# Talking-heads attention with a squared-ReLU FFN: GpSimd queue in written order, weights in eight spread loads, longer score bursts, column-tiled work bundled

## The chip, the cores and the metric

The kernel runs on one core of one Trainium2 chip. The metric is the device time of one execution in microseconds, the median of several runs. All times "us from the start" are from a profiled run's first instruction. With one core there is no second die to compare; a run is called slow when it is more than 1.5% above the fastest run of the same kernel. PE is TensorE, DVE VectorE, ACT ScalarE, POOL GpSimd, and SP the engine whose queue issues the gathers and stores. A name such as h_ps stands for the matmuls that write this PSUM tile.

## The reference

```python
scores = scale * np.matmul(q, k.transpose(0, 1, 3, 2))     # 8 batches, 12 heads, 448 x 64
scores = np.einsum('bhij,hg->bgij', scores, w_pre)         # mixes the heads
scores = scores - np.max(scores, axis=-1, keepdims=True)
attn = np.exp(scores)
attn = attn / (np.sum(attn, axis=-1, keepdims=True) + 1e-09)
attn = np.einsum('bhij,hg->bgij', attn, w_post)            # mixes them again
x = np.matmul(attn, v)                                     # -> (3584, 768)
h = np.maximum(x @ w_in, 0.0)                              # w_in 768 x 2048
out = h * h @ w_out                                        # w_out 2048 x 768
```

## The kernel before

A batch is cut into 45 steps of ten query rows. A step mixes the heads (`mix`: one matmul on a gathered tile G, an exp on ScalarE, a reciprocal on DVE, a normalising operation d on GpSimd) and, three steps later, mixes them back (`unmix`: four matmuls, a copy `at` on DVE). G is gathered by a DMA from the scores S, in written order six steps ahead; it has eight buffers (`AHEAD + 2`). The FFN of a batch is cut into units that serve as filler between the steps of the next batch. "share" spreads what is left of them over the rest of the batch, and single units (transposes, attention-value) are booked as debt in `owed`.

```python
LAG = 3; AHEAD = 6
...
def fill(ns):
    owed[0] += ns
    while filler and owed[0] > 0:
        w, f = filler.pop(0)
        f()
        owed[0] -= w
    if not filler:
        owed[0] = min(owed[0], 0.0)
...
with tc.manual_schedule(engines={PE}):            # the other queues are ordered by the framework
    ...                                           # transposes and scores of the first block
    for x in range(AHEAD):
        gather(steps[x])
    nc.gpsimd.dma_start(out=wpost_bf[:, :], in_=w_post[0:H, 0:H])
    vs[0] = load(v, 0, "v", 2)
    for c2 in range(NPAIR):                       # six loads of w1
        nc.gpsimd.dma_start(out=w1[c2][:, :], in_=moe_w_in[c2 * 128:(c2 + 1) * 128, 0:DFF])
    kk = load(k, 1, "kst", 1)
    staged[1] = (load(q, 1, "qst", 1), kk)
    for ft in range(FT):                          # sixteen loads of w2
        nc.gpsimd.dma_start(out=w2[ft][:, :], in_=moe_w_out[ft * 128:(ft + 1) * 128, 0:DMODEL])
    for i in range(len(steps) + LAG):
        ...
        rest = NT - (s0[1] if s0 else 0)
        share = sum(w for w, _ in filler) / max(rest - 1, 1) / 2 if s0 else 1e9
        now = timed.pop(i, [])
        if s0: mix(s0)
        for w, f in now:
            f()
            owed[0] -= w
        fill(share)
        if s1: unmix(s1)                          # queues attention-value units for i+1, i+2
        if i + AHEAD < len(steps): gather(steps[i + AHEAD])
        ...                                       # score bursts of two pairs at tiles 0, 2, 4
        fill(share)
```

The softmax here doesn't subtract the row's maximum and nothing guards it: scores larger than these inputs give would overflow.

Of the kernel before, what the change touches and what calls it, by code (L numbers as in the profile page):

```python
# [8 lines left out]
BF16 = mybir.dt.bfloat16  # L9
# [3 lines left out]
PE = mybir.EngineType.PE  # L13
# [17 lines left out]
LAG = 3  # L31
# [6 lines left out]
def kernel(  # L38
# [27 lines left out]
    def load(src, b, name, bufs, parts=1):  # L66
        t = stage.tile([P, H, R, D], BF16, name=name, tag=name, bufs=bufs)
        n = H // parts
        for x in range(parts):
            hs = slice(n * x, n * x + n)  # L70
            nc.gpsimd.dma_start(out=t[0:PR, hs, :, :].rearrange("p h r d -> p h (r d)"),
                                in_=src[b, hs, :, :].rearrange("h (p r) d -> p h (r d)", r=R))
        return t

    staged, vs = {}, {}
    kk = load(k, 0, "kst", 1, parts=3)
    staged[0] = (load(q, 0, "qst", 1, parts=3), kk)

    ident = consts.tile([P, P], BF16, name="ident")
    masks.make_identity(nc, ident[:, :])  # L80

# [35 lines left out]
    w1 = [wts.tile([P, DFF], BF16, name=f"w1_{c2}") for c2 in range(NPAIR)]  # L117
    w2 = [wts.tile([P, DMODEL], BF16, name=f"w2_{ft}") for ft in range(FT)]
# [64 lines left out]

    def ffn1_unit(b, ft):
        ps = bank("h_ps")
        for c2 in range(NPAIR):
            nc.tensor.matmul(ps[:, 0:S], lhsT=w1[c2][:, ft * 128:(ft + 1) * 128], rhs=xts[b][:, c2, :],  # L187
                             start=(c2 == 0), stop=(c2 == NPAIR - 1))
# [18 lines left out]
    def ffn2_unit(b, mt, nt, part):  # L207
# [3 lines left out]
        for ft in range(8 * part, 8 * part + 8):  # L211
            for n2 in ((nt,) if mt < 3 else (0, 1)):
                dst = ps[:, 0:384] if mt < 3 else ps[64 * n2:64 * n2 + 64, 0:384]
                nc.tensor.matmul(dst, lhsT=h2ts[(b, ft)][:, mt * 128:mt * 128 + ROWS[mt]],  # L214
                                 rhs=w2[ft][:, n2 * 384:(n2 + 1) * 384], start=(ft == 0), stop=(ft == FT - 1))
# [25 lines left out]
    def score_burst(b, blk, pairs):  # L241
# [12 lines left out]
        for h, ps in got:  # L254
            if h % 2 == 0:
# [64 lines left out]
    with tc.manual_schedule(engines={PE}):  # L320
        for _, f in turn_units(0):
            f()
        for x in range(3):
            score_burst(0, 0, [2 * x, 2 * x + 1])
        for x in range(AHEAD):
            gather(steps[x])
        nc.gpsimd.dma_start(out=wpost_bf[:, :], in_=w_post[0:H, 0:H])
        vs[0] = load(v, 0, "v", 2)
        for c2 in range(NPAIR):
            nc.gpsimd.dma_start(out=w1[c2][:, :], in_=moe_w_in[c2 * 128:(c2 + 1) * 128, 0:DFF])  # L330
        kk = load(k, 1, "kst", 1)
        staged[1] = (load(q, 1, "qst", 1), kk)
        for ft in range(FT):
            nc.gpsimd.dma_start(out=w2[ft][:, :], in_=moe_w_out[ft * 128:(ft + 1) * 128, 0:DMODEL])
        for i in range(len(steps) + LAG):
            s0 = steps[i] if i < len(steps) else None
            s1 = steps[i - LAG] if i >= LAG else None
            if s0:
                b, t = s0
                blk, tl = divmod(t, TPB)  # L340
                if t == 0:
                    if b == 0:
                        at_step(i + 12, (100, cg_unit))
                    at_step(i + 13, (900, lambda b=b: bias_unit(b)))
                    if b + 1 < B:
                        for x, u in enumerate(turn_units(b + 1)):
                            at_step(i + 15 + 3 * x, u)
                if t == 36 and b + 2 < B:
                    kk = load(k, b + 2, "kst", 1)
                    staged[b + 2] = (load(q, b + 2, "qst", 1), kk)  # L350
                if t == 10 and b + 1 < B:
                    vs[b + 1] = load(v, b + 1, "v", 2)
# [9 lines left out]
            if s1:  # L362
                unmix(s1)
                b1, t1 = s1
                if t1 % TT == TT - 1:
                    for x, u in enumerate(av_units(b1, t1 // TT)):
                        at_step(i + 1 + x, u)
                if t1 == NT - 1:
                    filler.extend(ffn_units(b1))
            if i + AHEAD < len(steps):  # L370
                gather(steps[i + AHEAD])
            if s0:
                nxt = blocks.index((b, blk)) + 1
                first = [0, 2, 4] if blk < 3 else [0, 1, 2]
                if nxt < len(blocks) and tl in first:
                    x = first.index(tl)
                    score_burst(*blocks[nxt], [2 * x, 2 * x + 1])
# [36 lines left out]
```

## Time and profile before

| what | before |
|---|---|
| median of the first three runs | 685.85 us (685.82 to 686.61) |
| busy share of PE, DVE, ScalarE, GpSimd | 89, 62, 59, 56% |
| first mix (m_ps) | 27.1 us |
| first FFN matmul (h_ps) | 120.3 us |
| seven batch periods, first h_ps of batch 0 to that of batch 7 | 523.0 us |
| from there to the end | 41.5 us |

The last three rows add to the span. They are a start that ends with the first FFN matmul, seven periods in which attention of one batch and FFN of the previous one run together, and the last FFN alone. The boundaries are the starts of the first h_ps of each batch in the PE timeline.

### The profile page before, as it was taken

The page shows a single profiled execution, that of the slowest core. Times are in us where ns is not written, and L with a number is a line of the kernel's source. Part 1 is how long each engine was busy: PE and PEld are TensorE (multiplying, and loading weights), DVE is VectorE, ACT ScalarE, POOL GpSimd, SP SyncE. Part 2 cuts the span into 40 slices and gives each one's busy share as a digit, 9 for nine tenths or more (in the row PEclk, how much of TensorE's full clock was granted, in tenths as well). Part 3 has the DMA queues.
Part 4 walks back from the last instruction along what each step waited for, and adds up shares of the span by engine and source line. Part 5 has one row for each costly group of instructions (what it writes and reads, how often), then busy time and mean ns, then how long its engine had stood idle before and what let it go on. Part 6 is the DMA issues. An engine that isn't in the chain of part 4 may idle for free.

```text
span 684.8 us, 16963 instructions
## 1 busy us (share of the span) xinstructions
PE 609.3 (89%) x6282; PEld 367.6 (54%) x6282; DVE 426.0 (62%) x1036; ACT 404.5 (59%) x1185; POOL 382.5 (56%) x545
## 2 busy tenths in 40 slices
PE   4207977899999999999999999999999999999897
PEld 3004544466556555566656565566556565556554
DVE  4105887566677767766767767666767667675201
ACT  2205777575477656775577657775577557764330
POOL 6226455576377734874376725873387436764360
PEclk9555898999999999999999999999999999999999
DMA  9999495548474665649474766549474345434102
GB/s 149 219 201 180 75 153 96 100 65 132 110 135 79 91 139 113 116 70 154 107 132 71 95 137 119 101 76 158 110 127 72 71 87 109 72 58 96 36 0 82
DMA packets 87959, 73.47 MB, mean 107 GB/s; under 512 B 5700, under 2 KB 84036, under 8 KB 87876
## 3 DMA queue, kind: packets, MB, share of 16 engines
q1 hardware_dynamic: 51842, 49.57, 34.4%
q0 software_dynamic: 35904, 22.81, 24.4%
q8 instruction: 49, 0.80, 0.5%
q14 instruction: 34, 0.28, 0.1%
q10 hardware_dynamic: 130, 0.01, 0.0%
HBM read 45.63 MB, written 11.01 MB: 83 GB/s over the span
## 4 chain that ended last, share of the span: by engine, by line
PE 71%; DMA 17%; DVE 6%; ACT 3%; issue 1%; POOL 1%; SPq 0%; DVEq 0%; ACTq 0%; POOLq 0%
PE o_ps L214 20%; PE h_ps L187 18%; DMA G<-S 10%; PE at_ps L296 9%; PE m_ps L276 8%; PE ot_ps L170 6%; PE s_ps L251 5%; DMA qst<-in_q_dram 5%; PE tr_ps L144 3%; DVE at L298 3%; DVE S L258 2%; DMA out_dram<-osb 2%; ACT xt L178 1%; PE vs_ps L157 1%; DMA w<-in_moe_w_out_dram 1%
## 5 line engine op out<-in xcount | busy, mean ns | idle before, releaser
L283 POOL TENSOR_SCALAR d<-e_sb,rc 120x448 bf16<-120x448 f32 x360 | 228.5, 638 | 202.7 <-DVE rc L281 200.6
L298 DVE CAST at<-at_ps 112x480 bf16<-112x480 f32 x360 | 231.4, 651 | 86.5 <-PE at_ps L296 83.3
L279 ACT ACTIVATE e_sb<-m_ps 120x448 f32<-120x448 f32 x360 | 195.9, 547 | 146.3 <-PE m_ps L276 98.0
L187 PE MATMUL h_ps<-xt,w 128*128 128x448 bf16 x768 | 164.9, 354 | 0.0
L214 PE MATMUL o_ps<-w,h 128*128 128x384 bf16 (+1 forms) x1024 | 162.6, 327 | 0.0
L296 PE MATMUL at_ps<-post,d 120*128 120x120 bf16 (+1 forms) x1440 | 138.6, 220 | 22.6 <-POOL d L283 22.2
L276 PE MATMUL m_ps<-G,pre 120*120 120x448 bf16 x360 | 135.8, 377 | 25.4 <-DMA G<-S 25.0
L296 PEld LDWEIGHTS <-d 120*128 120x128 bf16 (+1 forms) x1440 | 104.5, 101 | 69.2 <-POOL d L283 26.7
L192 POOL TENSOR_TENSOR h<-hr 128x448 bf16<-128x448 f32 x128 | 119.2, 931 | 34.9 <-ACT hr L191 34.3
L214 PEld LDWEIGHTS <-h 128*128 128x128 bf16 (+1 forms) x1024 | 85.0, 101 | 54.9 <-issue 7.4
L258 DVE CAST S<-s_ps 128x448 bf16<-128x448 f32 x192 | 109.8, 614 | 3.3 <-DMA G<-S 1.6
L191 ACT ACTIVATE hr<-h_ps 128x448 f32<-128x448 f32 x128 | 69.6, 544 | 65.2 <-PE h_ps L187 60.9
L281 DVE RECIPROCAL rc<-sm 120x1 f32<-120x1 f32 x360 | 57.1, 159 | 81.6 <-ACT e_sb L279 78.3
L256 ACT CAST S<-s_ps 128x448 bf16<-128x448 f32 x192 | 92.5, 540 | 21.7 <-PE s_ps L251 21.7
L187 PEld LDWEIGHTS <-w 128*128 128x128 bf16 x768 | 70.6, 98 | 62.3 <-issue 8.8
L276 PEld LDWEIGHTS <-pre 120*120 120x120 bf16 x360 | 48.8, 136 | 67.7 <-DMA G<-S 37.1
L279 ACT ACTIVATION_READ_ACCUMULATOR e_sb<-m_ps 120x1 f32 x360 | 73.9, 205 | 0.0
L251 PE MATMUL s_ps<-kT,qT 64*128 64x448 bf16 x384 | 60.5, 375 | 1.3 <-ACT e_sb L279 0.4
L170 PE MATMUL ot_ps<-at,v 112*64 112x150 bf16 x1152 | 48.7, 236 | 12.3 <-DVE at L298 12.2
L178 ACT ACTIVATE xt<-ot_ps,bvec 128x150 bf16<-128x150 f32 (+1 forms) x144 | 44.9, 383 | 22.5 <-PE ot_ps L170 22.5
L221 DVE COPY osb<-o_ps 128x384 f32<-128x384 f32 x48 | 26.7, 556 | 49.6 <-PE o_ps L214 48.8
L170 PEld LDWEIGHTS <-v 112*64 112x64 bf16 x1152 | 41.2, 113 | 21.9 <-issue 13.4
(33 smaller groups left out, 159.6 us busy)
## 6 DMA issues: line engine op xcount, KB each, us to landing
G<-S SPq DMA_DIRECT2D x352, 105.0 KB
v<-in_v_dram POOLq DMA_DIRECT2D x8, 672.0 KB, 10.1
kst<-in_k_dram POOLq DMA_DIRECT2D x7, 672.0 KB, 8.2
qst<-in_q_dram POOLq DMA_DIRECT2D x7, 672.0 KB, 13.2
w<-in_moe_w_in_dram POOLq DMA_DIRECT2D x6, 512.0 KB, 15.9
w<-in_moe_w_out_dram POOLq DMA_DIRECT2D x16, 192.0 KB, 7.4
out_dram<-osb SPq DMA_DIRECT2D x8, 336.0 KB
out_dram<-osb SPq DMA_DIRECT2D x8, 288.0 KB
```

The source lines that it names most:

```text
L170: nc.tensor.matmul(ps[64 * hh:64 * hh + 64, TQ * y:TQ * y + TQ], lhsT=vs[b][0:PR, g, r, :], rhs=at[0:PR, r, g, :], start=(y == 0 and r == ...
L187: nc.tensor.matmul(ps[:, 0:S], lhsT=w1[c2][:, ft * 128:(ft + 1) * 128], rhs=xts[b][:, c2, :], start=(c2 == 0), stop=(c2 == NPAIR - 1))
L192: nc.gpsimd.tensor_tensor(out=h2[:, :], in0=hr[:, :], in1=hr[:, :], op=ALU.mult)
L214: nc.tensor.matmul(dst, lhsT=h2ts[(b, ft)][:, mt * 128:mt * 128 + ROWS[mt]], rhs=w2[ft][:, n2 * 384:(n2 + 1) * 384], start=(ft == 0), stop ...
L251: nc.tensor.matmul(ps[:, 0:S], lhsT=qTs[b][rs, p, BLK_START[blk]:BLK_START[blk] + P], rhs=kTs[b][rs, p, :], start=True, stop=True)
L256: nc.scalar.copy(out=sb[:, h, :], in_=ps[:, 0:S])
L258: nc.vector.tensor_copy(out=sb[:, h, :], in_=ps[:, 0:S])
L276: nc.tensor.matmul(ps[0:n, 0:S], lhsT=pre[0:n, 0:n], rhs=Gs.pop(s)[0:n, :], start=True, stop=True)
L279: nc.scalar.activation(out=e[0:n, :], in_=ps[0:n, 0:S], func=ACT.Exp, scale=SCALE, accum_out=sm[0:n, 0:1])
L283: nc.gpsimd.tensor_scalar(out=d[0:n, 0:S], in0=e[0:n, :], scalar1=rc[0:n, 0:1], scalar2=-1.0 / S, op0=ALU.mult, op1=ALU.add)
L296: nc.tensor.matmul(ps[:, RG * r:RG * r + RG], lhsT=d[0:n, PR * r:PR * r + P], rhs=post[0:n, :], start=True, stop=True)
L298: nc.vector.tensor_copy(out=ats[(b, third)][0:PR, :, :, IQ * tl:IQ * tl + IQ], in_=ps[0:PR, 0:R * RG].rearrange("p (r g i) -> p r g i", r= ...
```

## The change

Its intent is to free the GpSimd queue of weight loads that stand before compute work, to spread these loads over two batches, and to switch PE less often between full, row-tiled and column-tiled matmuls. Cut to its core:

```diff
-LAG = 3
+LAG = 4
...
+    load(staged[0][0], q, 0, 0, 4)               # k and q parts alternate
+    for x in (4, 8):
+        load(staged[0][1], k, 0, x, x + 4)
+        load(staged[0][0], q, 0, x, x + 4)
...
-    w1 = [wts.tile([P, DFF], BF16, name=f"w1_{c2}") for c2 in range(NPAIR)]
-    w2 = [wts.tile([P, DMODEL], BF16, name=f"w2_{ft}") for ft in range(FT)]
+    w1 = [wts.tile([P, NPAIR, DFF // 4], BF16, name=f"w1_{x}") for x in range(4)]
+    w2 = [wts.tile([P, FT // 4, DMODEL], BF16, name=f"w2_{x}") for x in range(4)]
...
-            if h % 2 == 0:
+            if h % 2 == 0 or (b == 0 and h in (3, 9)):
                 nc.scalar.copy(out=sb[:, h, :], in_=ps[:, 0:S])
...
-    with tc.manual_schedule(engines={PE}):
+    with tc.manual_schedule(engines={PE, POOL}):
...
+        for x in range(2):                       # block 1 is scored before the steps
+            score_burst(0, 1, [3 * x, 3 * x + 1, 3 * x + 2])
...
+        at_load(0, load_v, 0)
+        at_load(2, load_k, 1)
+        at_load(5, load_q, 1)
+        for x in range(4):
+            at_load(10 + 5 * x, load_w1, x)
+            at_load(44 + 4 * x, load_w2, x)
+        for b in range(B):
+            if b + 1 < B:
+                at_load(NT * b + 32, load_v, b + 1)
+            if b + 2 < B:
+                at_load(NT * b + 36, load_k, b + 2)
+                at_load(NT * b + 40, load_q, b + 2)
...
-                    at_step(i + 13, (900, lambda b=b: bias_unit(b)))
+                    at_step(i + 16 + LAG, (900, lambda b=b: bias_unit(b)))
-                            at_step(i + 15 + 3 * x, u)
+                            at_step(i + 16 + LAG if x < 3 else i + 31 + LAG, u)
...
-                    for x, u in enumerate(av_units(b1, t1 // TT)):
-                        at_step(i + 1 + x, u)
+                    for u in av_units(b1, t1 // TT):
+                        at_step(i + 2, u)
                 if t1 == NT - 1:
-                    filler.extend(ffn_units(b1))
+                    at_step(i + 2, (0, lambda b1=b1: filler.extend(ffn_units(b1))))
...
-                first = [0, 2, 4] if blk < 3 else [0, 1, 2]
+                first = [0, 4] if blk < 3 else [0, 2]
-                    score_burst(*blocks[nxt], [2 * x, 2 * x + 1])
+                    score_burst(*blocks[nxt], [3 * x, 3 * x + 1, 3 * x + 2])
```

More of the change, by code (lines that the diff above doesn't have):

```diff
@@ L12 @@
 ALU = mybir.AluOpType
-PE = mybir.EngineType.PE
+PE, POOL = mybir.EngineType.PE, mybir.EngineType.Pool
 B, H, S, D = 8, 12, 448, 64
@@ L62, in bank, with stage_tile, load @@
         return psp.tile([P, 512 if dtype == F32 else 1024], dtype, name=name, tag="ps")
-    def load(src, b, name, bufs, parts=1):
-        t = stage.tile([P, H, R, D], BF16, name=name, tag=name, bufs=bufs)
-        n = H // parts
-        for x in range(parts):
-            hs = slice(n * x, n * x + n)
-            nc.gpsimd.dma_start(out=t[0:PR, hs, :, :].rearrange("p h r d -> p h (r d)"),
-                                in_=src[b, hs, :, :].rearrange("h (p r) d -> p h (r d)", r=R))
-        return t
+    def stage_tile(name, bufs):
+        return stage.tile([P, H, R, D], BF16, name=name, tag=name, bufs=bufs)
+    def load(t, src, b, h0=0, h1=H):
+        nc.gpsimd.dma_start(out=t[0:PR, h0:h1, :, :].rearrange("p h r d -> p h (r d)"),
+                            in_=src[b, h0:h1, :, :].rearrange("h (p r) d -> p h (r d)", r=R))
     staged, vs = {}, {}
-    kk = load(k, 0, "kst", 1, parts=3)
-    staged[0] = (load(q, 0, "qst", 1, parts=3), kk)
+    staged[0] = (stage_tile("qst", 1), stage_tile("kst", 1))
+    load(staged[0][1], k, 0, 0, 4)
     ident = consts.tile([P, P], BF16, name="ident")
     masks.make_identity(nc, ident[:, :])
+    load(staged[0][0], q, 0, 0, 4)
+    for x in (4, 8):
+        load(staged[0][1], k, 0, x, x + 4)
+        load(staged[0][0], q, 0, x, x + 4)
     def wcol(w, name, eng):
@@ L182, in av_units, with load_v, load_k, load_q @@
         return [(800, lambda cp=cp: av_unit(b, third, cp)) for cp in range(2)]
+    def load_v(b):
+        vs[b] = stage_tile("v", 2)
+        load(vs[b], v, b)
+    def load_k(b):
+        kst = stage_tile("kst", 1)
+        load(kst, k, b)
+        staged[b] = (stage_tile("qst", 1), kst)
+    def load_q(b):
+        load(staged[b][0], q, b)
+    def load_w1(x):
+        n = DFF // 4
+        nc.gpsimd.dma_start(out=w1[x][:, :, :],
+                            in_=moe_w_in[:, n * x:n * x + n].rearrange("(c p) f -> p c f", p=P))
+    def load_w2(x):
+        n = DFF // 4
+        nc.gpsimd.dma_start(out=w2[x][:, :, :],
+                            in_=moe_w_out[n * x:n * x + n, :].rearrange("(c p) m -> p c m", p=P))
     def ffn1_unit(b, ft):
@@ L186, in ffn1_unit @@
         for c2 in range(NPAIR):
-            nc.tensor.matmul(ps[:, 0:S], lhsT=w1[c2][:, ft * 128:(ft + 1) * 128], rhs=xts[b][:, c2, :],
+            nc.tensor.matmul(ps[:, 0:S], lhsT=w1[ft // 4][:, c2, ft % 4 * 128:ft % 4 * 128 + 128], rhs=xts[b][:, c2, :],
                              start=(c2 == 0), stop=(c2 == NPAIR - 1))
@@ L214, in ffn2_unit @@
                 nc.tensor.matmul(dst, lhsT=h2ts[(b, ft)][:, mt * 128:mt * 128 + ROWS[mt]],
-                                 rhs=w2[ft][:, n2 * 384:(n2 + 1) * 384], start=(ft == 0), stop=(ft == FT - 1))
+                                 rhs=w2[ft // 4][:, ft % 4, n2 * 384:(n2 + 1) * 384], start=(ft == 0), stop=(ft == FT - 1))
         if part == 0:
@@ L319 @@
     steps = [(b, t) for b in range(B) for t in range(NT)]
-    with tc.manual_schedule(engines={PE}):
-        for _, f in turn_units(0):
-            f()
+    with tc.manual_schedule(engines={PE, POOL}):
+        first = turn_units(0)
         for x in range(3):
+            first[2 * x][1]()
+            first[2 * x + 1][1]()
             score_burst(0, 0, [2 * x, 2 * x + 1])
+        for x in range(2):
+            score_burst(0, 1, [3 * x, 3 * x + 1, 3 * x + 2])
         for x in range(AHEAD):
@@ L327, with at_load @@
         nc.gpsimd.dma_start(out=wpost_bf[:, :], in_=w_post[0:H, 0:H])
-        vs[0] = load(v, 0, "v", 2)
-        for c2 in range(NPAIR):
-            nc.gpsimd.dma_start(out=w1[c2][:, :], in_=moe_w_in[c2 * 128:(c2 + 1) * 128, 0:DFF])
-        kk = load(k, 1, "kst", 1)
-        staged[1] = (load(q, 1, "qst", 1), kk)
-        for ft in range(FT):
-            nc.gpsimd.dma_start(out=w2[ft][:, :], in_=moe_w_out[ft * 128:(ft + 1) * 128, 0:DMODEL])
+        loads = {}
+        def at_load(i, f, *args):
+            loads.setdefault(i, []).append(lambda: f(*args))
+        at_load(0, load_v, 0)
[10 more added lines that the diff above has]
+                at_load(NT * b + 40, load_q, b + 2)
         for i in range(len(steps) + LAG):
+            for f in loads.get(i, []):
+                f()
             s0 = steps[i] if i < len(steps) else None
@@ L343 @@
                         at_step(i + 12, (100, cg_unit))
-                    at_step(i + 13, (900, lambda b=b: bias_unit(b)))
+                    at_step(i + 16 + LAG, (900, lambda b=b: bias_unit(b)))
                     if b + 1 < B:
                         for x, u in enumerate(turn_units(b + 1)):
-                            at_step(i + 15 + 3 * x, u)
-                if t == 36 and b + 2 < B:
-                    kk = load(k, b + 2, "kst", 1)
-                    staged[b + 2] = (load(q, b + 2, "qst", 1), kk)
-                if t == 10 and b + 1 < B:
-                    vs[b + 1] = load(v, b + 1, "v", 2)
+                            at_step(i + 16 + LAG if x < 3 else i + 31 + LAG, u)
             rest = NT - (s0[1] if s0 else 0)
@@ L373 @@
                 nxt = blocks.index((b, blk)) + 1
-                first = [0, 2, 4] if blk < 3 else [0, 1, 2]
-                if nxt < len(blocks) and tl in first:
+                first = [0, 4] if blk < 3 else [0, 2]
+                if 1 < nxt < len(blocks) and tl in first:
                     x = first.index(tl)
-                    score_burst(*blocks[nxt], [2 * x, 2 * x + 1])
+                    score_burst(*blocks[nxt], [3 * x, 3 * x + 1, 3 * x + 2])
             if i + 1 < len(steps) + LAG:
```

## The prediction

> **What bounds the kernel now.** I read the stretch table first (busy time of each engine in windows), with the cuts set where the first FFN matmul of each batch stands in the PE timeline: 120.3, 197.0, 272.4, 347.5, 423.5, 499.3, 574.5 and 643.3 us. The columns are stretch, length, busy us of PE, PEld, DVE, ACT, POOL, granted clock, DMA share, GB/s.
>
> ```profile
> 17.00:53.00 36.00, 4.17 (x12) 0.96 (x12) 3.64 (x9) 4.03 (x11) 9.13 (x18) 0.52 1.14 208
> 53.00:120.00 67.00, 54.54 (x604) 32.55 (x605) 52.40 (x138) 48.13 (x149) 37.36 (x58) 0.82 0.71 124
> ...
> 423.50:499.30 75.80, 73.64 (x789) 44.73 (x787) 53.17 (x129) 50.07 (x149) 45.92 (x65) 1.00 0.62 110
> ...
> 643.30:685.00 41.70, 36.83 (x226) 20.42 (x224) 3.90 (x7) 9.62 (x19) 14.92 (x16) 0.99 0.12 34
> ```
>
> So there are four regimes, not one bound. From 17 to 53 us every compute engine is nearly idle and only the DMA engines are full. From 53 to 120 us no engine is full; VectorE (DVE) is the busiest, 52.4 of 67 us. From 120 to 643 us, seven batch periods, PE is 97% busy and is the bound. The last 41.7 us are the last batch's FFN alone. The page's 89% for PE averages over these.
>
> Second view, the waits between 14 and 60 us, and the POOL timeline there:
>
> ```profile
> PE at_ps L296 <- POOL d L283: 19.0, 1, 19.0
> ACT e_sb L279 <- POOL d L283: 18.9, 1, 18.9
> PEld L276 <- DMA G<-S: 16.4, 4, 11.1
> ```
>
> ```profile
> 32.35 0.53 POOL L334 DMA_DIRECT2D w<-in_moe_w_out_dram x1 [2.15 <-DMA w<-in_moe_w_in_dram]
> 39.47 0.53 POOL L334 DMA_DIRECT2D w<-in_moe_w_out_dram x1 [6.59 <-DMA kst<-in_k_dram]
> 44.75 0.53 POOL L334 DMA_DIRECT2D w<-in_moe_w_out_dram x1 [4.76 <-DMA qst<-in_q_dram]
> ...
> 52.35 0.53 POOL L334 DMA_DIRECT2D w<-in_moe_w_out_dram x1 [0.41 <-DMA w<-in_moe_w_out_dram]
> 52.91 1.86 POOL L283 TENSOR_SCALAR d<-e_sb,rc 120x448 bf16<-120x448 f32 x3
> ```
>
> The reader should see a queue blocked at its head: four exps are done by 34.4 us, but the d operation that normalises them stands in the GpSimd queue behind sixteen w2 issues, each of which waits for an earlier load to land. With three e_sb buffers, ScalarE stops too, and PE after it. Before that, the first gather (issued at 18.14 us) lands only at 27.1 us, since the loads have filled the DMA engines.
>
> Third view, the PE timeline in the PE-bound regime (start us, duration, instructions):
>
> ```profile
> 437.02 0.35 PE L276 MATMUL m_ps<-G,pre 120*120 120x448 bf16 x1
> 437.21 0.37 PE L296 MATMUL at_ps<-post,d 120*128 120x120 bf16 x4
> 437.52 0.55 PE L251 MATMUL s_ps<-kT,qT 64*128 64x448 bf16 x4
> 438.00 0.40 PE L276 MATMUL m_ps<-G,pre 120*120 120x448 bf16 x1
> 438.33 0.58 PE L144 MATMUL tr_ps<-ident,kst 112*64 112x112 bf16 x16
> 438.85 0.38 PE L296 MATMUL at_ps<-post,d 120*128 120x120 bf16 x4
> ```
>
> ```profile
> 394.04 0.97 PE L170 MATMUL ot_ps<-at,v 112*64 112x150 bf16 x24 [0.81 <-DVE at L298]
> ```
>
> Read start to start, since busy times overlap. An m_ps takes 0.19 us before a full-array matmul but 0.33 (typically 0.28) before a column-tiled one; sixteen transposes take 0.52 us before a full-array matmul, but 0.42 where another column-tiled group follows. Hence a column-tiled group standing alone costs about 0.09 us in and 0.10 out, 0.19 in all. A score burst (64 rows) shows the same: at_ps to s_ps is 0.31 against 0.21, and four score matmuls take 0.48 where two pitches of 448 columns (0.19 each, as six h_ps take 1.14) would be 0.38; 0.10 on each side, 0.20 per burst. Last, an attention-value group waits up to 0.8 us for the at copy of the step just before it.
>
> **What the Trainium skill says.** "TensorEngine Tiling (Array Packing)", Key Properties: "Mode switching requires drain". The trace agrees, with the 0.09 to 0.10 us above at each side. "PSUM — Partial Sum Buffer", Engine vs sequencer instructions: the GpSimd queue is a strict FIFO; that is the 19.0 us wait. "DMA: Bandwidth & Descriptors", Queues, rings and completion order: each DMA engine goes round between the queues it has work for, a packet at a time. The trace agrees only in part: gathers do get through while loads run, but in 17 to 53 us at a DMA share of 1.14 the first took 9 us, against 2.9 us for the one at 79.45 us in the chain of waits.
>
> **The change, part by part.**
> (1) Start. k and q parts now alternate, and the two first score blocks are computed before the steps. From 1.3 us the first k part landed at 5.4, and four parts had by 10.24, so 1.6 us a part; the sixth lands near 13.4. Its transposes and copies (0.75 + 0.62), then four score matmuls and their copies (about 1.3) put the first block's S at 16.3 us, against 18.0 now. Fewer loads compete, so a gather of about 3 us gives the first mix at 19 us rather than 27.1.
> (2) The GpSimd queue in written order. Eight weight loads of 768 KB stand between steps, so no d waits for weights. This deletes the 34.4 to 52.9 stall, about 18.5 us, and the 12 us of slow first gathers around it.
> (3) Batch 0's own pace. From mix 10 at 59.7 us to mix 50 at 115.9 the kernel takes 1.40 us a step. DVE's 52.4 us of those 67 lose the copies of block 1 (now before the steps) and two copies per block (h 3 and 9, to ScalarE): fourteen at 0.53 us (six took 3.27 us) are 7, though four more steps come into the stretch, at 0.8 each. So DVE needs some 48 us for 50 steps, 0.97 a step. The DMA engines must bring 45 gathers of 105 KB (4.7 MB), five loads of v, k and q for batches 1 and 2 (3.4 MB) and w1 (3.1 MB): 11.2 MB, at 208 GB/s (the full stretch above) 54 us. With two bundles, each some 4 us of PE work in which ScalarE and DVE run short, I take 1.22 us a step, 61 us for 50 steps. First FFN matmul at 19 + 61 = 80 us instead of 120.3: 40 us gained.
> (4) Steady batches. Column-tiled groups go from 13 a batch (bias 1, transposes 6, attention-value 6; one adjacent already) to 3 bundles: 9 x 0.19 = 1.7 us. Score bursts go from 12 to 8: 4 x 0.20 = 0.8. The attention-value wait, 12.2 us in 16 waits over eight batches, is 1.5 a batch; with two steps between I count 1.2 as gone. Sum 3.7 a batch; all of it is on PE, which sets the end here. Six periods give 22, the last one (fewer groups) 2: 24 us of 523.
> (5) Given back. Bursts of six of the eight PSUM banks and bundles that open six must wait for copies (three at about 0.44 on ScalarE, three at 0.53 on DVE, beside the exps and at copies), and w2's 3.1 MB arrive in batch 1. I put 5 us for the seven periods. LAG 4 lengthens nothing but the drain of one step.
> (6) The end: 96 and 128 matmuls alone, 41.5 us, unchanged.
> Sum: 80 + (523 - 24 + 5) + 41.5 = 625.5; the reference time is 1 us above the profiled span, but (1) and (3) lean slightly careful, so I say 624.
>
> **The rivals.**
> A: batch 0 becomes DMA-bound. The loads merely move from one clump to a belt along the whole batch, gathers land late (6 to 9 us against six steps of lookahead, that is 7 us), and the pace stays at 1.4 to 1.5 us. For it: the share of 1.14 under loads, and the 7.7 us gather at 95.6 us while v, k and q arrive. Against: w1 isn't needed before step 50 and can lag. The first FFN matmul would be at 90 to 95, the total 636 to 641.
> B: PSUM stalls eat the steady gain. Six banks at once leave two; if each of 64 bursts costs PE 0.4 us, that is 26 us, and the total is 645. For it: PE already waits at bursts now (0.16 to 0.28 us where two bursts follow closely in batch 0). Against: ScalarE and DVE are at 66 and 70% in the steady stretch, and at the PE-bound pace of 1.68 us a step three extra copies drain within two steps.
> C: batch 0 runs at the pace of DVE alone and nothing is given back: first FFN matmul at 70, periods 3.8 shorter: 70 + 499 + 41 = 610.
> D: nothing moves, since the 18.5 us stall only shifts a DMA bound: the weights still have to land before w1 is used. It would give 660 to 685. Against: all weights landed by 60 us, w1 is used at 120, so there's room.
>
> **Range and chances.** The start stall is sure to go, and even A with B keeps 25 us. Between C with some luck (606) and A with half of B (648) should lie 8 of 10. Faster by over 2% means under 672; only D threatens it: 0.96 faster, 0.03 same, 0.01 slower.
>
> **What would show each step.** (1) and (2): first m_ps near 19 us; no d waiting over 3 us for a load; PE's stretch from 20 to 60 us over 50% busy. (3): first h_ps at 74 to 92 us; if later, look at waits on G (A) or at DVE's share. (4): periods near 72 us, tr_ps, vs_ps and ot_ps contiguous in the PE timeline, "PE ot_ps <- DVE at" below 3 us. (5): waits of s_ps, m_ps or tr_ps for DVE or ScalarE copies of 5 us in all, not 26. (6): the last 128 + 96 matmuls as now. I would be wrong if periods stay at 75 us, or if the first FFN matmul comes after 100.

## The result

The changed kernel takes 660.73 us (median of four runs: 660.58, 670.95, 660.88, 657.29; the second is a slow run, at a granted clock of 0.934 against 0.956 to 0.971). The kernel before took 685.84 us in the same rounds. The ratio of the fast runs is 0.9627, 95% interval 0.9572 to 0.9683: faster by 3.7%. A ratio here is the mean time of one kernel's fast runs over that of the other's in the same rounds, so it isn't quite the ratio of the medians quoted. The direction was right, but 660.7 lies outside the range of 606 to 648; 61.8 us of gain were forecast and 25.1 came.

| part of the span | before | predicted | after |
|---|---|---|---|
| first m_ps | 27.1 | 19 | 21.5 |
| first h_ps | 120.3 | 80 | 109.2 |
| seven periods | 523.0 | 504 | 508.2 |
| the rest | 41.5 | 41.5 | 41.4 |

So most of the miss, 27 of 37 us, is in one place, between the first mix and the first FFN matmul (61 us forecast, 87.7 measured). The stretch table of the changed kernel (columns as in the prediction) shows it:

```profile
21.50:45.00 23.50, 15.64 (x79) 7.98 (x80) 9.61 (x28) 11.25 (x36) 10.82 (x16) 1.00 0.92 157
45.00:65.00 20.00, 16.36 (x237) 10.95 (x234) 14.86 (x42) 14.55 (x47) 12.38 (x19) 0.91 1.03 195
65.00:85.00 20.00, 14.86 (x176) 10.15 (x173) 14.84 (x39) 12.82 (x43) 11.11 (x18) 0.83 0.94 154
85.00:109.20 24.20, 16.42 (x137) 9.83 (x138) 13.09 (x37) 13.54 (x43) 11.07 (x18) 0.65 0.97 180
...
405.10:479.10 74.00, 71.78 (x789) 44.90 (x787) 53.40 (x129) 49.74 (x150) 45.57 (x64) 1.00 0.62 114
```

No compute engine is full from 21.5 to 109.2 us: DVE, the limit that the prediction named, is busy for 13 of 24 us at 85 to 109, and PE for at most 16.4 of 20. What stands near its limit is the DMA share, the last number but one, 0.92 to 1.03 throughout. In the kernel before it was 1.14 from 17 to 53 us and 0.71 on average from there to 120. The clock falls to 0.65 in the last stretch. The Trainium skill, "TensorE: Matmul & The Clock Gate", Part 1, states that the array goes to half clock after an idle window of about 3.4 us. This trace agrees only in part: the clock was at half from 84.9 to 102.0 us, but in the 3.4 us before that PE was busy for 1.54 us and had no gap over 1.01.

The waits of the changed kernel in its first 130 us (waiter, releaser, us in total, times, longest) show what took the place of the weights:

```profile
PEld L299 <- DMA G<-S: 30.6, 25, 6.0
PE m_ps L299 <- DMA G<-S: 22.2, 16, 5.8
...
PEld L319 <- POOL d L306: 3.1, 3, 1.3
```

The wait of PE's weight loads for d, in the kernel before 24.2 us with 19.5 in the one stall, is 3.1. The wait of PE for gathers is 22; in the kernel before it was 7 from 53 to 120 us, after the stall, and 14 before that, most of it for the first gather. The chain that ended last, between 17 and 112 us, consists of the gathers for 57%. Its longest pieces (start us, us) are:

```profile
29.58 9.87 DMA G<-S
...
40.19 9.76 DMA G<-S
...
61.45 8.60 DMA G<-S
...
83.75 8.78 DMA G<-S
...
93.23 13.16 DMA G<-S
```

In these pieces a gather of 105 KB takes 8.6 to 13.2 us from issue to use, while loads run; over gathers 9 to 59 the mean is 9.8. The very first, with no load in flight (v's was issued at 6.69 us and its last packet came before), was issued at 17.64 us and used at 21.48. From the ninth on, a gather was never issued before the mix eight steps back had freed its G buffer. So eight steps take one such time to land (9.8 us), plus 2.3 us on average from the free buffer to the issue and 0.5 for the mix: 12.6 us, or 1.6 a step. The pace seen is near it, and the PE timeline has it:

```profile
97.73 0.63 PE L299 MATMUL m_ps<-G,pre 120*120 120x448 bf16 x1
...
108.66 0.39 PE L299 MATMUL m_ps<-G,pre 120*120 120x448 bf16 x1
...
109.19 1.30 PE L210 MATMUL h_ps<-xt,w 128*128 128x448 bf16 x6
```

The first of these is the 51st m_ps, so 50 steps take 76.2 us, 1.52 a step. The second is the 59th, and only behind it does the first FFN matmul stand, 11.5 us after the 51st.

Last, the bundle in the PE timeline of the changed kernel, with the same reading as in the prediction (start us, duration):

```profile
275.41 0.35 PE L299 MATMUL m_ps<-G,pre 120*120 120x448 bf16 x1
275.69 0.92 PE L158 MATMUL vs_ps<-onescol,v 112*64 112x1 bf16 x48
276.47 0.56 PE L145 MATMUL tr_ps<-ident,kst 112*64 112x112 bf16 x16
276.87 0.56 PE L145 MATMUL tr_ps<-ident,qst 112*64 112x112 bf16 x16
277.26 0.56 PE L145 MATMUL tr_ps<-ident,kst 112*64 112x112 bf16 x16
277.66 1.74 PE L171 MATMUL ot_ps<-at,v 112*64 112x150 bf16 x48
279.33 0.38 PE L319 MATMUL at_ps<-post,d 120*128 120x120 bf16 x4
```

Inside the bundle a transpose group takes 0.40 us start to start, against the 0.52 of a single one. The bundles do what they were made for.

### The profile page after: what moved, and what is told of

The parts are those of the page before. It is cut to its first block, busy times and chain, and to the rows that moved or that the text cites. A ratio compares the mean times of both kernels' runs of the same rounds, so it can differ in the third digit from the quotient of the medians.

```text
span 658.8 us, 16952 instructions
## 1 busy us (share of the span) xinstructions
PE 605.0 (92%) x6282; PEld 375.7 (57%) x6282; DVE 422.4 (64%) x1029; ACT 404.0 (61%) x1193; POOL 374.6 (57%) x531
## 4 chain that ended last, share of the span: by engine, by line
PE 71%; DMA 18%; ACT 4%; DVE 3%; SPq 2%; issue 1%; POOL 0%; ACTq 0%; DVEq 0%; POOLq 0%
PE h_ps L210 22%; PE o_ps L237 18%; DMA G<-S 15%; PE m_ps L299 9%; PE at_ps L319 8%; PE ot_ps L171 5%; PE s_ps L274 5%; PE tr_ps L145 3%; DMA out_dram<-osb 2%; ACT e_sb L302 2%; PE vs_ps L158 1%; DVE at L321 1%; ACT S L279 1%; SPq L293 1%; DMA qst<-in_q_dram 1%
## 5 line engine op out<-in xcount | busy, mean ns | idle before, releaser
L319 PEld LDWEIGHTS <-d 120*128 120x128 bf16 (+1 forms) x1440 | 111.9, 102 | 53.6 <-issue 8.0
L215 POOL TENSOR_TENSOR h<-hr 128x448 bf16<-128x448 f32 x128 | 119.2, 931 | 14.8 <-ACT hr L214 14.8
L237 PEld LDWEIGHTS <-h 128*128 128x128 bf16 (+1 forms) x1024 | 86.6, 101 | 52.4 <-issue 3.2
L210 PEld LDWEIGHTS <-w 128*128 128x128 bf16 x768 | 73.0, 98 | 60.2 <-issue 5.1
L281 DVE CAST S<-s_ps 128x448 bf16<-128x448 f32 x184 | 103.4, 615 | 4.8 <-PE s_ps L274 2.8
L279 ACT CAST S<-s_ps 128x448 bf16<-128x448 f32 x200 | 94.1, 552 | 16.0 <-PE s_ps L274 15.8
L299 PEld LDWEIGHTS <-pre 120*120 120x120 bf16 x360 | 48.8, 136 | 71.2 <-DMA G<-S 41.5
L302 ACT ACTIVATION_READ_ACCUMULATOR e_sb<-m_ps 120x1 f32 x360 | 76.5, 213 | 0.0
L179 ACT ACTIVATE xt<-ot_ps,bvec 128x150 bf16<-128x150 f32 (+1 forms) x144 | 42.7, 390 | 36.7 <-PE ot_ps L171 36.7
L171 PEld LDWEIGHTS <-v 112*64 112x64 bf16 x1152 | 43.7, 120 | 3.3 <-issue 2.7
## 6 DMA issues: line engine op xcount, KB each, us to landing
v<-in_v_dram POOLq DMA_DIRECT2D x8, 672.0 KB, 10.8
w<-in_moe_w_in_dram POOLq DMA_DIRECT2D x4, 768.0 KB, 11.1
w<-in_moe_w_out_dram POOLq DMA_DIRECT2D x4, 768.0 KB, 11.2
```

The source lines that it names most:

```text
L171: nc.tensor.matmul(ps[64 * hh:64 * hh + 64, TQ * y:TQ * y + TQ], lhsT=vs[b][0:PR, g, r, :], rhs=at[0:PR, r, g, :], start=(y == 0 and r == ...
L210: nc.tensor.matmul(ps[:, 0:S], lhsT=w1[ft // 4][:, c2, ft % 4 * 128:ft % 4 * 128 + 128], rhs=xts[b][:, c2, :], start=(c2 == 0), stop=(c2 = ...
L215: nc.gpsimd.tensor_tensor(out=h2[:, :], in0=hr[:, :], in1=hr[:, :], op=ALU.mult)
L237: nc.tensor.matmul(dst, lhsT=h2ts[(b, ft)][:, mt * 128:mt * 128 + ROWS[mt]], rhs=w2[ft // 4][:, ft % 4, n2 * 384:(n2 + 1) * 384], start=(f ...
L279: nc.scalar.copy(out=sb[:, h, :], in_=ps[:, 0:S])
L281: nc.vector.tensor_copy(out=sb[:, h, :], in_=ps[:, 0:S])
```

## The experiments

Fourteen kernels ran. Each was compared with runs of the kernel before on the same chip (medians of these 685.65 to 687.74 us). "First h_ps" and "periods" are from the one profiled run of each kernel, as above, so small differences in them rest on single executions. The medians include one slow run of the change, one of e_ahead9 and one of the kernel before (691.38 us); the ratios don't.

| kernel | median us | ratio to before (95%) | first h_ps | periods |
|---|---|---|---|---|
| the change | 660.73 | 0.9627 (0.9572 to 0.9683) | 109.2 | 508.2 |
| p_loads | 667.84 | 0.9734 (0.9678 to 0.9791) | 109.0 | 516.4 |
| p_start_loads | 666.27 | 0.9693 (0.9630 to 0.9757) | 108.0 | 516.3 |
| p_work | 676.69 | 0.9872 (0.9799 to 0.9945) | 125.1 | 513.0 |
| e_fewload (wrong) | 651.88 | 0.9477 (0.9415 to 0.9538) | 99.5 | 509.0 |
| e_early | 661.15 | 0.9618 (0.9559 to 0.9678) | 113.2 | 506.1 |
| e_ahead9 | 653.41 | 0.9479 (0.9399 to 0.9560) | 103.6 | 506.8 |
| e_move | 659.54 | 0.9623 (0.9552 to 0.9694) | 105.8 | 510.7 |
| e_noowe | 662.11 | 0.9661 (0.9598 to 0.9723) | 104.1 | 518.3 |
| e_noload (wrong) | 626.37 | 0.9137 (0.9102 to 0.9172) | 85.5 | 497.6 |
| e_gap | 660.20 | 0.9601 (0.9559 to 0.9644) | 108.0 | 507.5 |
| e_burst2 | 658.01 | 0.9602 (0.9566 to 0.9637) | 108.6 | 505.2 |
| c_gap9 | 647.63 | 0.9404 (0.9363 to 0.9445) | 95.9 | 507.4 |
| c_gap9m | 645.27 | 0.9371 (0.9330 to 0.9411) | 87.2 | 512.0 |
| c_burst2 | 641.03 | 0.9342 (0.9306 to 0.9378) | 88.9 | 508.3 |

### Which part gave what: p_loads, p_start_loads, p_work

p_loads is the kernel before with the GpSimd order and the spread loads only:

```diff
-with tc.manual_schedule(engines={PE}):
+with tc.manual_schedule(engines={PE, POOL}):
+    at_load(...)   # the load schedule of the change, w1 and w2 in four pieces each
```

> The kernel before with the GpSimd queue in written order and the weights in eight spread loads, and nothing else (its start, lag, bursts and single units stay). If the gain at the start comes from the order and the spreading alone, the first h_ps comes near 110 to 114 us (108.0 with the changed start too) and the total is 668 to 674. If the new start is what matters, first h_ps stays above 116 and the total above 678.

It took 667.84 us, first h_ps at 109.0. The order and the spreading alone give 18 of the 25 us, and the whole of the gain at the start: even the first mix comes at 22.0 us, with the old start. The other 6.6 us of its profiled gain lie in the periods, 4.0 of them in the first. No run separates the written order from the spreading, or either from the new shape of the loads.

p_start_loads has the start of the change as well, that is, the change without bundles, long bursts and lag:

```diff
-LAG = 4
+LAG = 3
-    at_step(i + 16 + LAG if x < 3 else i + 31 + LAG, u)
+    at_step(i + 15 + 3 * x, u)          # likewise bias, attention-value and FFN as before
-    first = [0, 4] if blk < 3 else [0, 2]
+    first = [0, 2, 4] if blk < 3 else [0, 1, 2]
```

> The changed kernel without bundles and long bursts: score bursts of two pairs, lag 3, transposes, bias and attention-value units at the steps where they stood before; the start, the loads and the GpSimd order are those of the change. If bundling gives the steady gain (about 1.5 to 2 us a period), periods are 75 us again and the total is 668 to 674; first h_ps near 105 to 109 as in the change. If the bundles cost batch 0 more than they give, the first h_ps comes earlier than 105.

It took 666.27 us, just below the expected range, first h_ps at 108.0, periods 516.3. The new start is worth at most 1 to 2 us, and the intervals of the two ratios overlap. The step to the change is what bundling, lag and bursts give: 8 us in the periods of the profiled runs, 5.5 us in the medians, where again the intervals overlap.

p_work is the other half alone: the kernel before with `LAG = 4`, the bundles and the three-pair bursts, weights and queue untouched.

> The kernel before with the bundles, the bursts of three pairs and lag 4, and nothing else (weights and GpSimd order as before). Bundling alone: periods 1 to 2 us shorter as from p_start_loads to the change, total 674 to 680, first h_ps near 120. Rival: without the written GpSimd order the scheduler places d and loads worse and bundling gains nothing, 684 to 690.

It took 676.69 us, ratio 0.9872; at a threshold of 2% that is unclear, though the interval lies under 1. The first h_ps came 4.8 us later than before, the periods took 10 us less. The two halves multiply to 0.9872 x 0.9693 = 0.957, a slightly larger gain than the 0.9627 of both together; the intervals don't tell these apart.

### Why batch 0 is slow: e_fewload, e_early, e_ahead9, e_noload

Three theories were open: gathers land late because loads fill the DMA engines (L), gathers are issued late at block borders because the next block's S isn't copied yet (B), or PE and the vector engines are slower there than I thought.

e_fewload loads one piece of w1 and of w2 instead of four:

```diff
-            at_load(10 + 5 * x, load_w1, x)
-            at_load(44 + 4 * x, load_w2, x)
+            if x == 0:
+                at_load(10 + 5 * x, load_w1, x)
+                at_load(44 + 4 * x, load_w2, x)
-  lhsT=w1[ft // 4][...]                 # and w2[ft // 4]
+  lhsT=w1[0][...]
```

> The changed kernel with only one of the four w1 loads and one of the four w2 loads (piece 0 is used for all, so the result is wrong on purpose; the matmuls are the same in number and shape). Loads in batch 0 and the first steps of batch 1 lose 4.7 MB. Theory L (gathers land late because software loads fill the DMA engines): the first h_ps comes at 85 to 92 us instead of 109.2, total about 640. Theory B (gathers are issued late at block borders, since the next block's S is copied too late): the pace hardly moves, first h_ps at 105 to 109, total 656 to 661.

The first h_ps came at 99.5 us and the total was 651.88: 9.7 us of the start, right in sign for L and smaller than it foresaw; v, k and q still load in batch 0. B foresaw no gain and is hurt by it.

e_early tests B directly, with every burst three steps earlier:

```diff
+EARLY = 3
-            if s0:
-                nxt = blocks.index((b, blk)) + 1
+            if i + EARLY < len(steps):
+                be, te = steps[i + EARLY]
+                nxt = blocks.index((be, te // TPB)) + 1      # cut: burst as before, by te
-  at_step(i + 16 + LAG if x < 3 else i + 31 + LAG, u)
+  at_step(i + 16 + LAG, u)
```

> The changed kernel with every score burst three steps earlier (and all six transposes in the first bundle, which that needs); lookahead of the gathers is still six steps. Theory B: the queue's waits for S copies at block borders vanish and the first h_ps comes at 95 to 100 us, total 648 to 652. Theory L: first h_ps stays at 105 to 110, total 657 to 661, since each gather still takes about 9 us to land.

The waits of the gather queue for S are the thing B names. In the changed kernel, up to 110 us, the largest of the queue's own waits is

```profile
SPq L293 <- DVE S L281: 29.2, 5, 15.5
```

(15.5 us of it before the first gather). In e_early, from 18 us on, no wait for a DVE copy of S is among the leading ones, and the largest is

```profile
SPq L294 <- PE at_ps L320: 20.9, 18, 4.3
```

Yet the first h_ps came at 113.2 us, later than 109.2, and the total was 661.15. B falls as the cause. The trace has a small part of it: the 51st mix starts at 94.5 us, 3.2 earlier than in the change, but the eight steps to the 59th, behind which the first h_ps stands in both, take 16.1 us instead of 10.9.

e_ahead9 is e_early with `AHEAD = 9` (and eleven G buffers).

> As e_early, with gathers issued nine steps ahead instead of six (eleven G buffers). Theory L in its form 'latency over lookahead': the pace goes with 6/9, first h_ps at 85 to 92 us, total 636 to 645. Theory T (throughput: the gathers' share of the DMA engines is the limit, and more in flight only wait longer): no better than e_early.

Against e_early, from the same rounds, the first h_ps moved from 113.2 to 103.6 and the total from 661.15 to 653.41 us. More lookahead helps, so the time to land does matter; but a pace that goes with 6/9 would have given 30 us, and one that goes with the buffers, 8/11, 25, not 10. The time from issue to use grew little (10.8 to 11.1 us on average up to the 59th gather); what grew is the time from a free buffer to the issue (1.2 to 3.6 us). What holds the issue there was not followed up.

e_noload takes away the loads altogether: k, q, v of batch 0 and one piece of each weight, loaded at step 0, serve for everything.

```diff
-        at_load(2, load_k, 1)
-        at_load(5, load_q, 1)
-        for b in range(B): ...           # all later loads of v, k, q
-    src = staged[b][which]               # and vs[b]
+    src = staged[0][which]
```

> The changed kernel without any load after the first steps: k, q and v of batch 0 and one piece of w1 and of w2 serve for everything (wrong on purpose; same instructions on PE, DVE and ScalarE). If loads on the DMA engines are what holds batch 0 at 1.6 us a step, it now runs at 1.0 to 1.15 us a step and the first h_ps comes at 78 to 88 us, near the 80 predicted; the periods lose their waits at the border too, total 612 to 628. Rival: the pace is set by the gathers' own chain (issue, landing, six steps ahead) even without loads; first h_ps at 95 to 100 as with few loads, total about 645.

The first h_ps came at 85.5 us and the total was 626.37. From the first mix to the first h_ps, the stretch table of the changed kernel and then of e_noload:

```profile
21.50:109.20 87.70, 63.28 (x624) 38.91 (x625) 52.39 (x142) 52.15 (x164) 45.38 (x69) 0.84 0.96 172
109.20:179.60 70.40, 69.07 (x757) 43.10 (x755) 48.44 (x115) 45.49 (x135) 43.09 (x60) 1.00 0.70 127
```

```profile
24.30:85.50 61.20, 51.99 (x624) 32.06 (x625) 50.84 (x142) 51.65 (x165) 35.92 (x58) 0.97 0.52 102
85.50:155.70 70.20, 69.10 (x758) 43.15 (x755) 48.59 (x115) 45.14 (x134) 39.08 (x55) 1.00 0.45 83
```

The two run the same 624 matmuls, 142 DVE and nearly the same ScalarE instructions before the first h_ps. With a DMA share of 0.52 this takes 61.2 us and DVE and ScalarE are over 80% busy; at a share of 0.96 it takes 87.7. The span differs by 658.8 - 624.5 = 34.3 us, of which 23.7 stand before the first h_ps and 10.6 in the periods. From issue to use a gather takes 5.0 us on average here, against 9.8 (gathers 9 to 59). The rival, that the loads' issues on GpSimd hold up d, finds no support: PE's weight loads wait for d for only 3.1 us in the change. So loads account for the slow start.

### Does an earlier FFN help? e_move and e_noowe

e_move loads v, k, q for the next batches at steps 45, 48, 52 and w2 at 56 to 65, out of batch 0's way:

```diff
-            at_load(44 + 4 * x, load_w2, x)
+            at_load(56 + 3 * x, load_w2, x)
-  at_load(NT * b + 32, load_v, b + 1)
+  at_load(NT * b + (32 if b else 45), load_v, b + 1)     # k 36 -> 48, q 40 -> 52
```

> The changed kernel with v for batch 1 and k, q for batch 2 loaded at steps 45, 48, 52 instead of 32, 36, 40, and w2 at steps 56 to 65 instead of 44 to 56: batch 0 carries 2.0 MB less. Theory L (landing time under loads, k, q and v above all): steps 36 to 50 run near 1.1 us each, first h_ps at 96 to 102, but if the loads only bother the gathers later, in batch 1, where PE has work of the FFN to do meanwhile, total 648 to 654. Rival: the waits come back one for one in batch 1, total 658 to 662.

The first h_ps came 3.4 us earlier, and the total stayed at 659.54. Its stretches from first mix to first h_ps and on to the second batch's first h_ps are

```profile
22.00:105.80 83.80, 61.93 (x624) 38.29 (x625) 52.10 (x142) 52.27 (x164) 43.56 (x66) 0.88 0.84 151
105.80:179.60 73.80, 70.08 (x757) 43.03 (x755) 48.49 (x115) 45.91 (x135) 45.24 (x63) 1.00 0.83 155
```

Both kernels reach the second batch's first h_ps at 179.6 us. PE is idle for 3.7 us of e_move's second stretch and for 1.3 of the change's. The time moved with the loads, one for one.

e_noowe changes one line:

```diff
-            owed[0] = min(owed[0], 0.0)
+            owed[0] = 0.0
```

> The changed kernel with one line different: the debt of the filler is set to 0 while the filler is empty. In both kernels single units run in batch 0 are booked as debt (about 8.4 us), which the share has to pay back before the first FFN unit. If that is why the first h_ps comes some seven steps after step 50 (7.4 us in the change, 4.4 in the kernel before), it now comes at 101 to 104 us; since PE is idle a third of the time there, the total gains 2 to 4 us, 656 to 659. Rival: the first h_ps waits for xt or w1, and nothing moves.

The first h_ps moved to 104.1 as expected, behind the 53rd mix instead of the 59th, so the debt delays it by some 5 us. (The expectation misread the distance from step 50: it is 11.5 us in the change, not 7.4, and 5.0 here.) But the total was 662.11: no gain. The second batch's first h_ps came at 178.7, 0.9 us earlier than in the change, so the expectation about the total fell: FFN work that starts earlier was no gain where the attention steps wait for DMA in any case. The profiled run also lost time later, in periods with the clock at half from 321.9 to 332.1 and from 400.4 to 407.2 us; whether the line causes that is not shown.

### Why bundling gave less than counted: e_burst2 and e_gap

In two steady periods I added the distances from start to start of each kind of matmul group in the PE timeline, with the idle time before the next group set apart (before: 272.4 to 423.5 us, after: 256.7 to 405.1):

```
us in two periods      before   after
tr_ps                    6.01    4.78
ot_ps                   10.87   10.08
vs_ps                    1.71    1.56
m_ps                    20.84   19.68
s_ps                    12.39   12.72
all groups             147.27  143.60
idle                     3.81    4.61
```

Transposes, bias, attention-value and the m_ps before them save 3.3 us in two periods, 1.7 a period, as the switches counted. The score groups save nothing: their number fell by a third, but a burst of six sometimes takes 0.92 us instead of 0.67. And PE idles more.

e_burst2 is the change with two-pair bursts again:

```diff
-  first = [0, 4] if blk < 3 else [0, 2]
-  score_burst(*blocks[nxt], [3 * x, 3 * x + 1, 3 * x + 2])
+  first = [0, 2, 4] if blk < 3 else [0, 1, 2]
+  score_burst(*blocks[nxt], [2 * x, 2 * x + 1])
```

> The changed kernel with score bursts of two pairs again (three per block), all else as changed. Counting mode switches, the longer bursts save 0.8 us a period and this is 5 to 6 us slower. By the two steady periods of the trace, the s_ps groups took as long as before (12.7 against 12.4 us in two periods) and 1.5 us of waiting stood behind them; then it is the same within 2 us, or faster.

It took 658.01 us, ratio 0.9602 against the change's 0.9627 from another set of rounds: the same. No gain from long bursts shows.

e_gap asks whether PE idles because the FFN work of a batch is spread to end with that batch, while the next FFN work is ready only five steps later (two before):

```diff
             rest = NT - (s0[1] if s0 else 0)
+            if s0 and s0[1] < LAG + 2:
+                rest = LAG + 2 - s0[1]
+            elif s0 and s0[0] < B - 1:
+                rest += LAG + 2
```

> The changed kernel, where the FFN work of a batch is spread over six steps more (to the step at which the next batch's FFN work is ready) instead of ending with the batch; no instruction is added or removed. Theory G: bundling saved about 2 to 2.7 us of PE time a period, but readies the FFN work three steps later (lag 4 and two steps), and in those steps PE has no filler and idles (2 us in the last 8 of a period, against 0.8 before). Then periods fall from 74 to about 72, and the total to 645 to 652, with fewer dips of the clock. Rival: PE's idle time at the border is ordinary waiting for gathers that filler can't fill; total 658 to 661.

It took 660.20 us, the same as the change. The stretches around a period's end tell why. First the last 8.3 us of a period in the changed kernel, then the last two stretches of a period in e_gap:

```profile
323.00:331.30 8.30, 6.27 (x89) 4.18 (x90) 6.22 (x16) 6.44 (x22) 3.18 (x5) 1.00 0.57 130
```

```profile
308.00:317.00 9.00, 7.37 (x58) 4.49 (x56) 4.85 (x11) 3.94 (x11) 2.32 (x4) 1.00 0.93 188
317.00:326.80 9.80, 9.80 (x132) 6.45 (x130) 7.10 (x18) 5.26 (x17) 3.20 (x5) 1.00 0.54 145
```

The idle 2 us at the end are filled, as meant. But now 1.6 us are lost just before, while k and q load (DMA share 0.93). In the period before this one (waits from 230 to 243 us) the loss has a name:

```profile
DVE osb L244 <- DMA out_dram<-osb: 2.9, 1, 2.9
PE m_ps L299 <- DVE osb L244: 2.3, 1, 2.3
```

The FFN's last units now fall among the loads, and their copies wait for an output store to land and free its buffer. That is likely the same cause in another place, full DMA engines, but no run tests it.

### Put together: c_gap9, c_gap9m, c_burst2

c_gap9 is e_ahead9 with the lines of e_gap and e_noowe, which gave nothing by themselves.

> Everything that helped put together: nine steps of lookahead with early bursts, the FFN work spread to the next batch's, and no debt while the filler is empty. If the gains add: first h_ps near 98, periods 71 to 72, total 634 to 642. If they share one cause (idle PE at the border filled either way): 645 to 650.

It took 647.63 us, in the range named for one shared cause. Its ratio, 0.9404, is below e_ahead9's 0.9479, but the intervals overlap, so the extra gain of those lines is likely and not shown.

c_gap9m adds the later loads of e_move.

> As c_gap9, with v for batch 1, k and q for batch 2, and w2 loaded later (as in e_move, which alone moved waits from batch 0 into batch 1). If filler now covers the waits in batch 1: 2 to 4 us under c_gap9. If not: the same within 1 us.

It took 645.27 us, 2.4 us less in the same rounds; the intervals of the ratios overlap.

c_burst2 is c_gap9m with two-pair bursts.

> The fastest so far (c_gap9m, 645) with score bursts of two pairs. The same question where gathers wait less: if bursts of six banks cost PE waits for the copies, 1 to 4 us faster than c_gap9m's ratio of 0.937; if they save switches, 3 to 6 us slower.

It took 641.03 us, ratio 0.9342, interval 0.9306 to 0.9378. That is correct, 6.6% faster than the kernel before and the fastest that computes the right result. From c_gap9m to it the intervals overlap.

## Why the prediction was wrong, point by point

**Start, step (1): right, a little off.** The first mix came at 21.5 us, not 19: the gather took 3.8 us, not 3, and the first was issued at 17.64, 1.3 us after the forecast S. The new start itself hardly matters: with the old one p_loads has its first mix at 22.0.

**The GpSimd order, step (2): right.** The stall for d is gone, and the order with the spread loads gives 18 us alone (p_loads). What failed is the belief that its 18.5 us, and 12 more, would all reach the end.

**Batch 0's pace, step (3): this is the step that failed.** It said 1.22 us a step, 61 us for 50 steps, and a first h_ps right behind them, at 80. The runs showed 1.52 us a step, 76.2 us for 50 steps, and 11.5 us more to the first h_ps; with the 2.5 us of step (1) that is 109.2. Three terms were wrong:
- DVE was taken as the leading limit and the DMA engines as second at 11.2 MB and 208 GB/s, 54 us. From first mix to first h_ps they moved 87.7 us x 172 GB/s = 15.1 MB, since some two and a half pieces of w2 (2.0 MB) and fourteen more gathers (1.6 MB) belong into that time as well. And 208 GB/s was read from a stretch of mostly weight loads with rows of 1536 and 4096 B; the mix of this stretch runs at 172 at a share of 0.96. Even the 11.2 MB alone need 65 us at that rate. The trace's packet records say why: one engine needs 132 ns per KB for k, q and v (packets of 512 B), 100 for w2 (1536 B), and for w1 81 in the rows of the kernel before (4096 B) but 105 in those of the change (1024 B). w1 in its new shape thus costs the 16 engines 20.2 us instead of 15.5, though not all of that need be the shape: w2's rows are unchanged, and they went from 93 to 100. Without loads the same work takes 61.2 us (e_noload), which is the predicted 61 for fewer steps.
- The first h_ps doesn't follow step 50. The 51st m_ps starts at 97.7 and the first h_ps at 109.2, behind the 59th, in part because of the debt (e_noowe: behind the 53rd). Such a distance was there to be read in the kernel before, 115.9 to 120.3, behind the 57th.
- Time at the start was added to the end one for one. e_move and e_noowe show that this isn't so while the DMA engines are full: each brought the first h_ps forward, and the second batch's came within 1 us of when it did in the change.

**Steady periods, step (4): right in mechanism, too large in sum.** Bundling saved 1.7 us a period on PE groups, as counted; the attention-value wait for at fell from 8.8 us (125 to 600 us) to almost nothing. The score bursts' 0.8 us never came (e_burst2). But the sum of 508.2 us lies near the 504 forecast partly by luck: 6.6 of the 14.8 us saved come with the loads alone (p_loads), which this step did not forecast. Bundles, lag and bursts give 8 (p_start_loads to the change) to 10 us (p_work), where 24 less 5 were forecast; in the two steady periods above the change saves 1.35 us each (75.55 to 74.2).

**Given back, step (5): too small, for a reason that it didn't name.** The waits of s_ps and m_ps for ScalarE came to 4.4 us from 125 to 600 us, as forecast, but PE also idles longer at the period's end (2.0 us of the 8.3 shown above), and loads of k and q delay gathers there. Without loads the periods take 497.6. The clock dip in the second period (248 to 256 us, at 0.59 and 0.55) is part of it.

**The end, step (6): right**, 41.4 against 41.5 us.

**The rivals.** A, batch 0 becomes DMA-bound, is what happened, with the evidence that I had listed for it and set aside; it was too mild at 90 to 95 us and 636 to 641. Its counter-argument, that w1 can lag, fails because loads that lag still share the engines with the gathers. B's size didn't come. C, 70 and 610 us, isn't reached even without loads (e_noload: 85.5 and 626.4 us); those times are near the main forecast of 80 and 624. I had in effect predicted the kernel without its loads. D gave 660 to 685, and the result is at its edge. It named the wrong wait (no wait of h_ps for weights shows in the changed kernel's first 130 us), but it was right that a good part of the stall only moved a DMA bound. The prediction's own sign of being wrong, a first FFN matmul after 100 us, came.

Open: how the DMA engines' time splits between waiting for bandwidth and waiting in line. e_ahead9 shows that more gathers in flight get more through (181 GB/s against 174 in e_early from 21.5 to 100 us), but no run separates the two, and the profile gives no landing time for single gathers.

## What to carry to other kernels

When a stall is removed, ask which resource did the work during the stall: here the weights' bytes still had to come, and they met the gathers in the next 60 us. Add up the bytes that must move before the next dependent stage, and divide by a rate from a stretch with the same kinds of transfers; if the result is near the forecast for that stage, that resource sets it. Work moved earlier inside a stage that waits for something else gained nothing here in two tries, and fewer mode switches are worth what the groups beside them save only if the new grouping doesn't wait for buffers.

## What the Trainium skill lacked or had wrong

- "DMA: Bandwidth & Descriptors", Queues, rings and completion order, tells how queues share an engine, but not what that does to the time of a small transfer: a gather of 105 KB that takes 3.8 us from issue to use with no load in flight (17.64 to 21.48 us) takes 8.6 to 13.2 us in the chain beside loads of k, q, v and weights.
- The same page's Bandwidth section gives 341 GB/s for a 1 MB load from HBM. No page has a figure for loads that cast from fp32 to bf16 in rows of 512 to 1536 B beside such gathers; here the engines were full (share 0.96) at 172 GB/s. By the packet records a casting load takes 66 ns of one engine for a packet of 512 B, 105 for 1024 B, 149 for 1536 B, and in the kernel before 323 for 4096 B (sizes as written).
- "TensorEngine Tiling (Array Packing)", Key Properties, names the drain at a mode switch without a size. The runs show about 0.09 us into and 0.10 us out of a column-tiled group, and 0.12 us saved for each transpose group that has another behind it (0.52 against 0.40).
- "TensorE: Matmul & The Clock Gate" warns of waits longer than its window, and in another place of frequent short idling, without a size. In the changed kernel from 44 us to the last FFN the clock fell to half after five stretches of 3.4 us in which PE was busy for 1.40 to 1.93 us and had no gap over 1.52; it stayed full after all those with 1.99 us or more, and after one with 1.86.
